# A hand-written instruction order, searched anew for a load in two parts

## The chip, the cores and the metric

One core of a Trainium2 chip runs the kernel. The metric is the device time of one execution in microseconds (us); lower is better. A profile of one execution tells when each instruction ran on each engine: PE (TensorE), DVE (VectorE), ACT (ScalarE), POOL (GpSimd) and SP (SyncE, which issues DMAs here).

## The reference

A layer norm of x (2048 tokens of 512, bf16) feeds two branches whose sum is added to x. Branch A is attention with 32 heads of 16 in four segments of 512 tokens: causal softmax inside the segment, plus a memory read of all earlier segments, mixed by a gate for each head. Branch B is a dense layer of width 1792 with silu.

```python
xn = layernorm(x)                                    # 2048 x 512
q, k, v = xn @ wq, xn @ wk, xn @ wv                  # 32 heads of 16
for s in range(4):                                   # segments of 512 tokens
    p = softmax(qs @ ks.T * 16 ** -0.5 + mask)       # causal within the segment
    a_mem = (phi(qs) @ M) / (phi(qs) @ z + 1e-6)     # phi(t) = t + 1 for t > 0, else exp(t)
    outs.append(g * a_mem + (1 - g) * (p @ vs))      # g = sigmoid(beta), one for each head
    M += phi(ks).T @ vs; z += phi(ks).sum(0)
return x + concat(outs) @ wo + silu(xn @ w1) @ w2
```

## The kernel before

The work is cut into small pieces, and one string, ORDER, lists all 1,349 of them in the order in which they are recorded. Each engine runs its own instructions in exactly that order; nothing is moved by a scheduler. A loop at the end of the function takes the words one by one and calls the function that PIECES names for them. So ORDER alone decides what stands ahead of what in each engine's queue, and how far a producer runs ahead of its reader.

The pieces that are spoken of below, with s for the segment:

- xc, xd, xs, xg, xq, xi, Nv: layer norm of one token tile (sums at L286, variance at L289, square root on ACT at L303 or on POOL at L297 and L300, reciprocal at L306, normalising at L315). X turns a tile on PE (L845), Xa and Xv copy it out (L851), XD turns it by DMA (L857).
- k, q, v, h: products with wk, wq, wv, w1; one word is a quarter of a 128x512 result in segments 0 and 1, half of one in segments 2 and 3. In segment 0 a word of k, q or h is two matmuls of 256 columns. kv, ka, qv, qa, vv, va copy a result from PSUM (v on DVE, a on ACT; L376, L399, L406). kp (L385, POOL) and kf split k into odd and even heads. ha is the tanh half of silu (ACT, L492), hv the rest (DVE, L497).
- fp, fa, fv and gp, ga, gv: phi of k and of q on POOL (L417, called pos), ACT (L423, called ex) and DVE (L433); t turns phi of k by DMA.
- S: scores of one batch (PE, L724), its exp on ACT (L730) and its causal masks on POOL (L744). The number is 18 s + 9 pair + batch. E and O: the weighted sums of v for the even and odd heads of four (PE, L791), copied by Ev, Ov, Ea, Oa (L821, L828), which also send the softmax sums to the tile zraw by small DMAs (L813); Om merges them (L835).
- s, sv, r, w, R, W: sums, their reciprocals (L545, L560) and gate weights (L566); z and d spread these over rows by DMA (L577); zv, dv multiply with them (L589, L599); m, n, nv are the memory's products (nv adds at L608).
- o, oc, od, oh: products with w2 and wo for one output tile (L336 or L338); st and sh store it (L621, L668). In o3.1.17 the numbers are segment, output tile, and the piece of the sum (14 to 17 are the attention's four quarters, below that the dense branch). xl loads x for the last sum. lw0 and lw1 load w2 and wo through ACT's queue.

Scores use a PSUM tile (psS) of one buffer; all other results share four banks (tag pb), so a product waits until the copy of the result that held its bank is done. A product stands in whole 128-column form (L336) or as four 32-column matmuls side by side (L338), by what tiled piece comes next in ORDER:

```python
psS = psatt.tile([P, 4, L], F32, name="psS")        # psatt: bufs=1
def bank(shape, dtype, name):
    return pp.tile(shape, dtype, name=name, tag="pb")   # pp: bufs=4
```

The loads at the start go through SP in this order: x, wv, wk, wq, x tiles 4 to 7, w1 in two halves of its columns, x tiles 8 to 15, beta.

Of the kernel before, what the change touches and what calls it, by code (L numbers as in the profile page):

```python
# [47 lines left out]
S31 o0.0.5 o0.2.14 h1.13.0 h1.13.1 o0.2.16 gv1.2 h1.13.2 o0.1.16 h1.13.3 ha1.13 fv1.1 o0.0.9 fp1.0
S30 oc0.1.9.1 od0.1.8.0 fp1.2 o0.1.5 o0.1.4 st0.0 h1.12.0 h1.12.1 h1.12.2 hv1.13 Nv13 XD13 h1.12.3 ha1.12 hv1.12 t1.1 o0.1.11 o0.3.17 o0.1.12
S33 fa1.2 oc0.1.9.0 kp2.0 o0.3.14 od0.3.3.1 od0.2.11.1 st0.2 oc0.3.0.0 o0.3.13 o0.3.10 E6 o0.1.6 o0.3.7  # L50
S32 o0.3.16 od0.1.8.3 oc0.3.2.0 mw0.2 o0.3.9 O6 o0.1.13 fv1.2 Ev6 oc0.3.0.1 o0.3.8 t1.2 Ov6 fa1.0 o0.1.15 fv1.0 od0.1.8.2
S35 o0.1.17 gp1.3 v2.0.0 o0.1.7 ga1.3 t1.0 o0.3.12 q2.2.0 q2.2.1 qv2.2
S34 od0.3.3.0 v2.0.1 vv2.0 o0.3.6 od0.3.3.2 ga2.1 Om6 o0.1.0 o0.3.1 E7 Ev7 o0.1.1
S41 o0.3.4 h1.5.0 O7 gv1.3 h1.5.1 h1.5.2 Ov7 od0.1.8.1 h1.5.3 gp2.1 o0.3.5 ha1.5 oc0.3.2.1
S37 o0.1.14 o0.3.15 hv1.5 m1.2 mv1.2 od0.3.3.3 o0.3.11 st0.3 k3.1.0 s1 gv2.1 sv1 r1.0 k3.1.1 gp2.3 r1.2 kv3.1 ga2.3
S36 o0.1.2 oc0.1.3.0 q3.3.0 q3.3.1 v2.3.0 qa3.3 v2.3.1 vv2.3 r1.3 gp2.2 xl0.1
S40 o1.2.13 r1.1 oc1.2.3.1 q3.1.0 m1.0 mv1.0 mw1.0 od1.2.1.1 oc0.1.3.1 o0.1.10 st0.1 w1 d1.0 d1.2 q3.1.1 qv3.1 o1.2.2 ga2.2
S43 oc1.2.11.1 z1.2 h1.6.0 h1.6.1 h2.8.0 Om7 h2.8.1 o1.2.4 ha2.8 hv2.8 h1.6.2 h1.6.3 od1.2.1.2 ha1.6
S38 E8 hv1.6 o1.2.9 o1.2.0 gv2.3 h2.11.0 h2.11.1 ha2.11 o1.2.10 o1.2.8
S42 gv2.2 v3.3.0 v3.3.1 Ev8 fp2.0 v3.0.0 v3.0.1 hv2.11 fa2.3 vv3.0 dv1.2 d1.1 k3.0.0 d1.3 fa2.0 k3.0.1 kv3.0 vv3.3 zv1.2  # L60
S39 q3.2.0 q3.2.1 qa3.2 fv2.0 z1.3 oc1.2.11.0 fp2.3 E9 q3.0.0 Ev9
S44 q3.0.1 k3.2.0 qv3.0 oc1.2.3.0 O8 fa2.1 fv2.3 Ov8 k3.2.1 kv3.2
S45 v3.2.0 v3.2.1 o1.0.9 gp3.2 fp2.1 mw1.2 fa2.2 dv1.3 xl1.0 zv1.3 h2.7.0 h2.7.1 vv3.2 o1.0.6 ha2.7 hv2.7 xl1.2
S48 o1.0.13 oc1.0.7.0 o1.0.4 h2.6.0 h2.6.1 Om5 n1.3 ha2.6 o1.2.12 kp2.3 o1.2.7 nv1.3 od1.2.1.0 oc1.0.10.0
# [878 lines left out]
```

## Time and profile before

| | before |
|---|---|
| median of 3 runs | 221.3 us (220.81 to 221.44) |
| profiled execution, its own time | 220.8 us |
| its span, first to last instruction | 219.1 us |
| granted TensorE clock | 1.0 |
| instructions in the profile | 9,343 |

The span is what the profile shows between the first and the last instruction; 1.7 us of the profiled execution's time lie outside it. Rows of an engine give the busy share of 40 equal slices in tenths. Times in rows of the timeline are us from the span's start, then the duration, then engine, line, operation and what it writes and reads. Matmuls overlap, so a row's duration holds the tail of the last one; the distance between starts tells the rate.

### The profile page before, as it was taken

What the parts mean: (1) busy time and instruction counts of PE and PEld (TensorE: products, weight loads), DVE (VectorE), ACT (ScalarE), POOL (GpSimd) and SP (SyncE); (2) the same over time, 40 slices, a digit from 0 to 9 for tenths busy, and PEclk for the clock granted to TensorE, in tenths of its full rate; (3) what the DMA queues carried; (4) which work ended last, traced back from release to release, by engine and by line L of the source; (5) the groups of instructions that cost most, each with busy time, mean ns of one, the idle gap of its engine ahead of it and who ended that gap; (6) DMA issues with size and microseconds to landing.
All of it is one profiled execution on the core that took longest, in us unless ns stands there. A gap on an engine that the chain in (4) does not pass through costs nothing.

```text
span 219.1 us, 9343 instructions
## 1 busy us (share of the span) xinstructions
PE 211.6 (97%) x4019; PEld 116.3 (53%) x4042; DVE 181.0 (83%) x370; ACT 184.2 (84%) x173; POOL 126.8 (58%) x203
## 2 busy tenths in 40 slices
PE   7999999999999999999999999999999999999994
...
DVE  7899999999897878757988979777899798669364
ACT  3899989999999999999999999999999988860000
POOL 6039986679687845695845486667768473410000
...
GB/s 197 357 372 128 79 129 344 42 79 46 4 4 75 25 86 71 83 62 29 51 74 61 43 121 28 47 79 7 4 99 75 75 76 45 97 60 76 97 52 97
DMA packets 33273, 19.60 MB, mean 89 GB/s; under 512 B 14672, under 2 KB 33232, under 8 KB 33232
## 3 DMA queue, kind: packets, MB, share of 16 engines
...
q14 instruction: 10, 0.08, 0.1%
...
## 4 chain that ended last, share of the span: by engine, by line
PE 82%; DVE 9%; POOL 4%; issue 2%; ACT 1%
PE ps L336 20%; PE psO L338 16%; PE ps L338 15%; PE psS L724 9%; PE psO L336 9%; PE psV L791 8%; PE psS L338 4%; DVE stats L286 2%; POOL Pb L744 2%; DVE Vz L406 1%; POOL k L385 1%; DVE hT L497 1%; DVE pk L433 1%; POOL lows L744 1%; PE ptr L845 1%
## 5 line engine op out<-in xcount | busy, mean ns | idle before, releaser
L730 ACT ACTIVATE Pb<-psS 128x2048 bf16<-128x2048 f32 x72 | 135.2, 1877 | 6.3 <-PE psS L724 4.1
L744 POOL TENSOR_SCALAR_AFFINE_SELECT Pb<-Pb 128x512 bf16<-128x512 bf16 (+2 forms) x88 | 61.6, 710 | 19.2 <-ACT Pb L730 16.5
L497 DVE SCALAR_TENSOR_TENSOR hT<-th,ps 128x512 bf16<-128x512 bf16 x56 | 38.0, 681 | 10.6 <-ACT th L492 10.2
L744 POOL TENSOR_SCALAR_AFFINE_SELECT lows<-Pb 64x512 bf16<-64x512 bf16 (+1 forms) x40 | 23.2, 581 | 37.5 <-ACT Pb L730 31.1
L338 PE MATMUL psO<-w_sb,hT 128*32 128x512 bf16 (+2 forms) x708 | 43.3, 321 | 0.0
L336 PE MATMUL ps<-xnT,w_sb 128*128 128x512 bf16 (+1 forms) x165 | 34.2, 329 | 0.4 <-DVE Vz L406 0.2
L492 ACT ACTIVATE th<-ps 128x512 bf16<-128x512 f32 x56 | 33.2, 594 | 1.7 <-PE ps L338 1.6
L338 PEld LDWEIGHTS <-hT 128*32 128x32 bf16 x876 | 21.6, 97 | 14.0 <-issue 2.6
L338 PE MATMUL ps<-xnT,w_sb 128*32 128x512 bf16 (+1 forms) x448 | 26.4, 348 | 0.0
L724 PE MATMUL psS<-qT,k 32*128 32x64 bf16 (+3 forms) x512 | 23.0, 233 | 0.5 <-ACT Pb L730 0.3
L336 PEld LDWEIGHTS <-w_sb 128*128 128x128 bf16 x168 | 15.8, 98 | 11.4 <-issue 1.0
L791 PE MATMUL psV<-Pb,Vz 128*32 128x448 bf16 (+7 forms) x512 | 21.6, 286 | 0.2 <-POOL Pb L744 0.2
L724 PEld LDWEIGHTS <-k 32*128 32x128 bf16 x512 | 9.4, 92 | 22.8 <-issue 22.2
L336 PE MATMUL psO<-w_sb,hT 128*128 128x512 bf16 (+2 forms) x82 | 20.9, 326 | 0.6 <-issue 0.5
L791 PEld LDWEIGHTS <-Vz 128*32 128x32 bf16 x768 | 16.2, 97 | 9.2 <-issue 0.8
L621 DVE SCALAR_TENSOR_TENSOR o_out<-psO,x_res 128x512 bf16<-128x512 f32 x14 | 9.6, 689 | 6.6 <-PE psO L338 4.9
L338 PEld LDWEIGHTS <-w_sb 128*32 128x32 bf16 x448 | 11.2, 96 | 7.3 <-issue 1.6
L724 PE MATMUL psS<-qT,kT 16*128 16x448 bf16 (+3 forms) x256 | 14.7, 269 | 0.0
L821 DVE CAST oraw<-psV 128x512 bf16<-128x512 f32 x15 | 10.2, 682 | 3.1 <-PE psV L791 3.0
L406 DVE CAST Vz<-ps 128x512 bf16<-128x512 f32 x15 | 10.2, 682 | 2.8 <-PE ps L338 1.6
L336 PEld LDWEIGHTS <-hT 128*128 128x128 bf16 x89 | 7.8, 98 | 8.7 <-issue 2.2
L336 PE MATMUL ps<-xnT,wq_sb 128*128 128x256 bf16 (+1 forms) x59 | 12.1, 322 | 0.2 <-issue 0.2
...
## 6 DMA issues: line engine op xcount, KB each, us to landing
...
```

Of the source, the lines that this page charges most:

```text
L286: nc.vector.bn_stats(out=stats[t][:], in_=xs(t, t + 1)[:, 0, :])
L336: return [nc.tensor.matmul(out, lhsT=lhsT, rhs=rhs, start=start, stop=stop, skip_group_check=True)]
L338: nc.tensor.matmul(out[c : c + 32], lhsT=lhsT[:, c : c + 32], rhs=rhs, start=start, stop=stop, tile_position=(0, c), skip_group_check=True,)
L406: copy(out=Vzs[s % 2][:, j, :, 0:3:2, :], in_=sts[s].pop(("v", j))[:, :].rearrange("p (h r d) -> p h r d", r=2, d=DH),)
L492: nc.scalar.activation(out=th[:], in_=sts[s]["h", ft][:, :], func=AF.Tanh, scale=0.5)
L497: nc.vector.scalar_tensor_tensor(out=st["hT"][:, ft, :], in0=st.pop(("th", ft))[:], scalar=1.0, in1=st.pop(("h", ft))[:, :], op0=ALU.add, ...
L621: out = nc.vector.scalar_tensor_tensor(out=o_out[:], in0=st.pop(("psO", j)), scalar=0.5, in1=st["x", j][:], op0=ALU.mult, op1=ALU.add)
L724: nc.tensor.matmul(psS[:, g, c : c + q2 - q1], lhsT=keys[rows], rhs=st["qT"][rows, dt, q1:q2], start=True, stop=True, tile_position=(32 * ...
L730: exp = nc.scalar.activation(out=blocks(Pb, b).rearrange("p y g c -> p g y c"), in_=psS[:, :, :].rearrange("p g (y c) -> p g y c", c=BLOCK ...
L744: over[id(Pb)].append(nc.gpsimd.affine_select(out=out, in_=in_, compare_op=ALU.is_ge, fill=0.0, base=base, pattern=[[0, out.shape[1]], [1, ...
L791: nc.tensor.matmul(psV[32 * g : 32 * g + 32, q0 : q0 + nq].rearrange("p (y c) -> p y c", y=weights.shape[2]), lhsT=Vzs[s % 2][:, kt, 4 * d ...
L821: copy(out=oraw[:], in_=sts[s].pop(("psV", 0))[:, :])
```

## The change

Only ORDER changes: the same pieces in another order. A search over orders was run again with the loads as the kernel has them, w1 in two parts. Four copies change their engine: kv0.1 becomes ka0.1, qa3.2 and qa3.3 become qv3.2 and qv3.3, and Ev14 becomes Ea14 (a is ACT, v is DVE). The S words stand in the same order, and what stands between them differs in nearly every line. The diff, cut to the lines that matter:

```diff
--- before
+++ after
 ORDER = """
-kind odd omask ones0 ones1 zeros xc0 xd0 xc1 xq0 xi0 Nv0 busy44 xd1 xq1 xc2 xi1 X0.1 Nv1 xd2 Xa0.1 busy6 v0.0.0 v0.0.1 xq2 X1.1 Xa1.1 xs3 xi2 Nv2 v0.0.2 xq3 v0.0.3 xi3 v0.1.0 v0.1.1 Nv3 X2.1 va0.0 k0.0.0 k0.0.1 tb Xv2.1 X3.1 v0.1.2 v0.1.3 Xv3.1 vv0.1 k0.1.0 k0.0.2 k0.0.3 ka0.0 fp0.0 kf0.0 q0.0.0 q0.0.1 q0.0.2 q0.0.3 xs4 k0.1.1 qa0.0 k0.1.2 k0.1.3 kv0.1 fa0.0 xs7
-S0 k0.3.0 fa0.1 k0.2.0 k0.2.1 k0.2.2 k0.2.3 kv0.2 k0.3.1 k0.3.2 q0.1.0 xs5 xs6 xg4.4 fv0.0 k0.3.3 kv0.3
-S2 q0.1.1 v0.2.0 kp0.1 q0.1.2 q0.1.3 qv0.1 v0.2.1 v0.2.2 v0.2.3 vv0.2 fa0.2 Nv6 Nv4 XD6 XD4 h0.0.0 h0.0.1
-S1 Nv5 XD5 h0.0.2 h0.0.3 ha0.0 hv0.0 h0.1.0 h0.1.1 fp0.2 h0.1.2 h0.1.3 q0.2.0
-S3 q0.2.1 q0.2.2 q0.3.0 q0.3.1 q0.3.2 q0.2.3 Nv7 qv0.2 ha0.1 h0.2.0 h0.2.1 kp0.2 q0.3.3
-S4 qv0.3 hv0.1 XD7 fv0.2 fa0.3 h0.2.2 v0.3.0 v0.3.1 v0.3.2 t0.0 t0.2 xs10 h0.3.0 h0.3.1 h0.3.2 h0.4.0 fp0.3 h0.3.3 ha0.3 v0.3.3
-S7 vv0.3 fp0.1 hv0.3 h0.4.1 h0.4.2 h0.4.3 kp0.3 h0.2.3 v1.2.0 ha0.4 v1.2.1 xs13 tanh E0 Ev0
-S5 v1.2.2 v1.2.3 h0.5.0 hv0.4 h0.5.1 h0.5.2 ha0.2 h0.5.3 vv1.2 fv0.3 O0 Ov0
-S11 lw0 hv0.2 xs11 q1.1.0 q1.1.1 q1.1.2 v1.1.0 v1.1.1 v1.1.2 v1.1.3 q1.1.3 q1.2.0 lw1
-S6 vv1.1 q1.2.1 q1.2.2 q1.2.3 v1.3.0 v1.3.1 v1.3.2 qv1.1 ga1.1 xs8 qv1.2 v1.0.0 v1.0.1 xs9 xg8.4 v1.0.2 v1.0.3 vv1.0 v1.3.3 ha0.5 hv0.5 t0.3
...
-S13 q1.3.1 q1.3.2 Nv9 q1.3.3 qv1.3 k1.2.3 Nv11 XD11 h0.9.0 h0.9.1 Om1 h0.9.2 h0.9.3 h0.10.0 ha0.9 hv0.9 kv1.2 kp1.2
...
-S15 k1.1.2 h1.0.0 h1.0.1 h1.0.2 k1.1.3 h1.0.3 ha1.0 xs14 E2 kv1.1 XD10 Ev2
-S17 O2 Ov2 h1.10.0 h1.10.1 h1.10.2 kp1.1 xl0.2 m0.2 mv0.2 h1.10.3 m0.0 ha1.10 mv0.0 hv1.0 fp1.3
...
-S14 ha0.12 xs12 k2.1.0 hv0.11 Om0 gp1.0 h1.3.1 k2.1.1 kv2.1 hv0.12 q2.1.0 q2.1.1
-S16 xg12.4 k2.2.0 k2.2.1 h1.3.2 h0.13.0 qv2.1 kv2.2 h1.3.3 Om2 E3 ha1.3
...
-S24 hv0.13 o0.2.7 oc0.2.10.1 od0.2.11.2 fv1.3 h1.8.0 h1.8.1 Nv15 XD15 h1.8.2 h1.8.3 h1.11.0 h1.11.1 h1.11.2 ha1.8
...
-S23 h1.4.0 oc0.0.7.1 o0.2.9 o0.0.6 h1.4.1 o0.0.1 Nv12 Ov4 h1.4.2 h1.4.3 ha1.4 od0.0.0.1 o0.0.4 bmask gv1.0 od0.0.0.2
-S25 h1.9.0 h1.9.1 kp2.1 Om3 zv0.3 h1.9.2 XD12 h1.9.3 ha1.9 oc0.2.10.0 hv1.4 o0.2.12 XD14 E5 zv0.1 o0.2.15
...
-S51 n1.0 o1.2.15 h2.4.0 h2.4.1 ha2.4 od1.2.1.3 nv1.0 o1.0.14 od1.0.1.0 fv2.2 t2.3 t2.2 o1.2.14 o1.2.16 st1.2
-S50 k3.3.0 k3.3.1 ga2.0 hv2.4 kp3.0 kv3.3 ga3.2 O10 Ov10 od1.0.1.3 o1.0.15 st1.0 h2.2.0 h2.2.1 ha2.2 o1.1.9 hv2.2
-S52 h2.9.0 kp3.1 m2.0 h2.9.1 ha2.9 o1.1.13 mv2.0 o1.1.1 od1.1.6.0 gv3.2 gp2.0 E11 hv2.9
-S56 o1.3.8 oc1.3.4.1 od1.3.9.2 Om9 o1.3.7 o1.1.16 Ev11 o1.1.14 od1.1.6.1 O11 Ov11 o1.1.3 kp3.2 Om10 o1.3.2 ga3.0
...
-S64 o2.2.10 xl2.0 hv3.8 od2.0.6.3 s3 o2.0.17 o2.2.3 sv3 r3.1 dv2.1 h3.9.0 h3.9.1 ha3.9 od2.0.6.1 dv2.2 r3.0 od2.2.13.0
...
-S71 hv3.13 o2.1.12 o2.3.4 h3.3.0 o2.3.9 h3.3.1 h3.10.0 h3.10.1 ha3.3 oc2.3.5.0 ha3.10 o3.2.5 o3.2.11 hv3.3 oh1.0 oc2.1.0.1 o3.2.8 o3.2.7 hv3.10 h3.6.0 oh5.1 h3.6.1 ha3.6 xl3.0 od2.3.10.2 O15 R0.3 d3.1 oc2.1.0.0 o2.1.13 oh13.0 R0.0 Oa15 o3.2.1 R0.2 oh7.0 dv3.0 oc2.1.3.1 o3.2.0 o3.0.5 hv3.6 o2.3.6 oh2.1 o3.1.2 o3.1.7 dv3.1 oc3.0.0.0 o3.0.11 R0.1 W0 oh13.1 od2.3.10.0 o3.0.9 o2.1.1 oc2.1.3.0 o3.2.13 o3.2.10 dv3.3 od3.0.3.3 o3.1.13 o2.3.3 Om15 o3.1.8 o3.1.1 o2.3.14 od3.0.3.0 o2.3.16 o2.3.17 xl2.3 R1.3 o3.1.6 o3.1.9 z3.2 o3.0.13 R1.1 od3.1.0.0 od2.1.9.1 R1.0 R1.2 W1 oh6.0 o2.3.8 Om14 zv3.2 o3.0.8 oc3.0.0.1 oc3.1.10.1 o2.3.7 o2.1.11 oc3.0.12.0 o3.0.7 z3.0 dv3.2 oh0.1 z3.1 od2.1.9.0 o2.3.12 z3.3 o3.2.2 o2.1.8 o2.1.4 st2.1 o3.2.4 o2.3.1 od2.3.10.3 o3.2.12 o3.1.4 oc3.1.10.0 od3.0.3.1 n3.0 oc3.1.11.1 od2.3.10.1 od3.1.0.1 o2.3.13 zv3.0 oh10.0 nv3.0 xl3.1 o3.0.4 oc2.3.2.0 o3.2.3 o2.3.0 o3.0.14 o3.2.6 oc2.3.5.1 st2.3 n3.2 oh3.0 xl3.2 oh2.0 zv3.3 oh11.0 od3.1.0.2 oh10.1 nv3.2 o3.0.1 oc3.1.11.0 o3.1.12 zv3.1 oh9.1 o3.1.14 oh14.1 oc3.0.12.1 o3.2.9 oh8.1 n3.1 nv3.1 o3.2.14 o3.1.3 n3.3 oh14.0 o3.0.16 od3.0.3.2 oh4.1 oh0.0 o3.1.15 o3.2.16 oh5.0 o3.1.16 nv3.3 o3.0.2 o3.0.17 o3.0.6 o3.0.10 o3.0.15 st3.0 o3.2.17 o3.2.15 oh6.1 st3.2 od3.1.0.3 oh8.0 oh16.1 o3.1.17 o3.1.5 oh12.0 oh17.1 oh9.0 st3.1 oh7.1 oh15.0 oh17.0 oh4.0 oh16.0 sh0 oh12.1 oh3.1 oh15.1 oh11.1 oh1.1 sh1
+kind odd omask ones0 ones1 zeros xc0 xd0 xc1 xq0 xi0 Nv0 busy44 xd1 xq1 xc2 xi1 X0.1 Nv1 xd2 Xa0.1 busy6 X1.1 xq2 v0.0.0 v0.0.1 v0.0.2 Xa1.1 v0.1.0 v0.1.1 xs3 xq3 xi2 Nv2 v0.0.3 X2.1 xi3 Nv3 v0.1.2 X3.1 v0.1.3 Xv2.1 k0.0.0 tb k0.0.1 Xv3.1 k0.0.2 vv0.1 va0.0 k0.0.3 ka0.0 kf0.0 q0.0.0 xs4 xs7 q0.0.1 q0.0.2 q0.0.3 k0.1.0 qa0.0 bmask k0.1.1 k0.1.2 fa0.0 fp0.0 fv0.0 t0.0
+S0 k0.2.0 k0.2.1 xs6 xs5 xg4.4 k0.1.3 ka0.1 fp0.1 v0.2.0 v0.2.1 v0.2.2 q0.1.0 q0.1.1 q0.1.2 kp0.1
+S2 v0.2.3 fa0.1 k0.2.2 k0.2.3 k0.3.0 k0.3.1 kv0.2 k0.3.2 k0.3.3 q0.1.3 vv0.2 qv0.1 kv0.3 kp0.3 Nv6
+S1 h0.0.0 h0.0.1 h0.0.2 h0.0.3 XD6 h0.3.0 ha0.0 v0.3.0 v0.3.1 Nv5 XD5 v0.3.2 h0.1.0
+S3 Nv4 h0.1.1 h0.1.2 hv0.0 v0.3.3 vv0.3 h0.3.1 h0.3.2 XD4 h0.3.3 h0.2.0 ha0.3 h0.1.3 xs10 hv0.3
+S4 fv0.1 h0.2.1 h0.2.2 q0.3.0 q0.3.1 q0.3.2 q0.3.3 Nv7 q0.2.0 fp0.3 q0.2.1 q0.2.2 q0.2.3 ha0.1 XD7 t0.1 fa0.2 qv0.3
+S7 hv0.1 h0.4.0 qv0.2 h0.4.1 h0.4.2 h0.2.3 ha0.2 h0.4.3 kp0.2 xs9 fp0.2 E0 Ev0 v1.2.0
+S5 tanh v1.2.1 v1.2.2 hv0.2 xs11 v1.2.3 v1.1.0 v1.1.1 vv1.2 h0.5.0 v1.1.2 v1.1.3 vv1.1 ha0.4 hv0.4 xs8 xg8.4 h0.5.1
+S11 h0.5.2 h0.5.3 ha0.5 O0 q1.1.0 Ov0 q1.1.1 q1.1.2 q1.1.3
+S6 k1.2.0 k1.2.1 qv1.1 k1.2.2 ga1.1 hv0.5 lw0 fv0.2 v1.3.0 v1.3.1 q1.2.0 v1.3.2 v1.3.3 vv1.3 k1.2.3 kv1.2 Nv8 XD8 q1.0.0
...
+S13 k1.1.1 O1 Ov1 h0.9.0 h0.9.1 h0.9.2 h0.9.3 h0.10.0 ha0.9 xs15
...
+S15 h1.0.0 h1.0.1 xs13 kv1.1 h1.0.2 hv0.10 qv1.3 h1.10.0 h1.10.1 xl0.2 E2 Ev2 h1.0.3 ha1.0 hv1.0 h1.10.2 xs12
+S17 h1.10.3 k1.3.0 ha1.10 k1.3.1 k1.3.2 xg12.4 k1.3.3 kv1.3 O2 h0.12.0
...
+S14 lw1 h0.11.1 k2.2.0 k2.2.1 kv2.1 kv2.2 q2.1.0 q2.1.1 hv0.12
+S16 h1.3.0 h1.3.1 h1.3.2 kp1.2 qv2.1 h0.11.2 Om1 h0.11.3 m0.0 mv0.0 h1.3.3 ha1.3 ha0.11 Nv15 E3 Ev3
...
+S24 q2.3.0 q2.3.1 mw0.0 Ov3 Nv13 hv0.13 h1.8.0 h1.8.1 h1.8.2 h1.8.3 vv2.1 kp1.3 ha1.8 o0.2.7
...
+S23 xl0.0 h1.4.0 h1.4.1 o0.0.1 gp1.0 h1.4.2 od0.2.11.3 o0.2.17 od0.0.0.3 o0.0.4 h1.4.3 Om2 zv0.2 ga1.2 ha1.4 oc0.0.2.1 o0.2.12
+S25 o0.0.5 o0.2.16 hv1.4 h1.9.0 h1.9.1 h1.9.2 o0.0.11 oc0.0.7.0 o0.0.3 h1.9.3 ha1.9 gv1.0 E5 od0.2.11.0
...
+S51 o1.0.15 n1.0 xl1.1 t2.1 h2.4.0 h2.4.1 kp3.0 nv1.0 fa2.2 o1.2.16 o1.2.14 oc1.2.11.1 o1.2.7 st1.2 ha2.4 O10 xl1.3
+S50 k3.3.0 k3.3.1 Ov10 od1.0.1.2 h2.2.0 h2.2.1 hv2.4 xl1.0 ha2.2 o1.0.14 kv3.3 fv2.2
+S52 t2.2 o1.3.8 ga3.3 h2.9.0 od1.3.9.1 o1.3.0 kp3.2 od1.3.9.0 hv2.2 o1.3.13 o1.1.9 oc1.1.10.1 od1.3.9.2 od1.1.6.1 fv2.0 t2.0 h2.9.1 ha2.9 hv2.9
+S56 oc1.1.10.0 o1.1.5 gp2.0 o1.1.13 o1.3.1 o1.3.10 o1.1.11 ga2.0 oc1.0.10.0 st1.0 o1.1.1 E11 Ev11 o1.3.6 kp3.3 Om10
...
+S64 o2.0.3 hv3.8 o2.0.10 o2.0.14 n2.3 nv2.3 o2.0.12 od2.0.6.3 h3.9.0 h3.9.1 ha3.9 s3 oc2.0.5.0
...
+S71 o2.3.7 E15 Ev15 oc2.1.3.1 h3.10.0 h3.10.1 ha3.10 oc2.1.0.1 xl2.3 od2.3.10.0 hv3.10 o2.3.14 h3.6.0 Om14 h3.6.1 oh4.1 o2.3.0 ha3.6 oh7.0 oh0.1 o3.2.2 oh1.1 O15 o3.2.9 hv3.6 o3.2.5 oh2.1 Oa15 o2.3.9 o3.1.2 o3.1.5 o3.1.3 o3.1.9 xl2.1 dv3.2 o2.3.4 o3.0.5 o2.3.1 oc3.0.0.0 R0.2 od3.0.3.2 o2.1.15 od3.1.0.2 R0.3 R0.1 o3.1.12 oc3.1.10.0 R0.0 W0 z3.2 oc3.0.12.0 o2.3.6 o2.3.12 dv3.3 o3.0.7 dv3.1 o3.2.1 od3.1.0.1 oh9.1 R1.1 od3.0.3.0 z3.0 o2.1.14 oc2.3.2.0 oc3.0.0.1 R1.0 o2.3.17 o3.1.7 oc2.3.5.1 od2.3.10.3 oc3.1.10.1 o3.0.10 R1.2 o3.0.11 st2.3 oh0.0 o2.1.2 R1.3 oh7.1 o3.1.4 oh1.0 od2.1.9.2 o3.1.1 o2.1.10 o2.1.6 W1 oh12.1 n3.2 oh2.0 o3.0.6 oh8.0 zv3.2 o3.0.2 oh10.0 o3.2.11 od3.0.3.1 z3.3 z3.1 od3.0.3.3 od3.1.0.3 dv3.0 nv3.2 oh16.0 od2.1.9.3 zv3.0 o3.2.3 od3.1.0.0 o3.1.8 o3.1.16 o3.1.6 st2.1 xl3.2 o3.2.0 o3.1.13 oh10.1 n3.0 nv3.0 n3.3 xl3.3 oh4.0 o3.0.4 o3.0.1 o3.0.8 oh13.0 oh6.0 Om15 o3.2.10 o3.2.14 n3.1 o3.1.14 o3.0.16 o3.2.16 oh11.1 zv3.3 oh3.0 oh11.0 oh12.0 nv3.3 o3.1.17 o3.2.7 oh14.1 o3.0.9 oh9.0 oc3.1.11.1 oc3.0.12.1 zv3.1 nv3.1 o3.0.14 o3.1.15 o3.2.15 o3.0.17 oh17.0 o3.0.15 o3.0.13 st3.0 oc3.1.11.0 st3.1 oh14.0 oh15.0 o3.2.13 o3.2.4 oh5.0 o3.2.8 oh13.1 o3.2.12 o3.2.6 o3.2.17 sh0 st3.2 oh5.1 oh3.1 oh17.1 oh6.1 oh15.1 oh8.1 oh16.1 sh1
 """
```

More of the change, by code (lines that the diff above doesn't have):

```diff
@@ L48 @@
[L48 to L64, printed above, removed]
```

81 lines of the change are left out of this document (49 added, 32 removed).

## The prediction

> **What bounds the kernel now.** I read the profile's page first, then the costliest groups, the waits of PE, and the order of time in the stage where PE's row has its low digits.
>
> ```profile
> span 219.1 us, 9343 instructions
> PE 211.6 (97%) x4019; PEld 116.3 (53%) x4042; DVE 181.0 (83%) x370; ACT 184.2 (84%) x173; POOL 126.8 (58%) x203
> PE   7999999999999999999999999999999999999994
> DVE  7899999999897878757988979777899798669364
> ACT  3899989999999999999999999999999988860000
> POOL 6039986679687845695845486667768473410000
> ```
>
> PE is busy to the end; ACT is full until slice 34, DVE most of all in slices 3 to 12, POOL in slices 4 and 5. The ACT groups say what paces the list: 72 exps of 1.88 us, and beside each about one shorter piece.
>
> ```profile
> L730 ACT ACTIVATE Pb<-psS 128x2048 bf16<-128x2048 f32 x72 | 135.2, 1877 | 6.3 <-PE psS L724 4.1
> L492 ACT ACTIVATE th<-ps 128x512 bf16<-128x512 f32 x56 | 33.2, 594 | 1.7 <-PE ps L338 1.6
> L423 ACT ACTIVATE ex<-kT 128x512 bf16<-128x512 bf16 x12 | 7.4, 622 | 0.0
> ```
>
> The scores tile psS has one buffer, so a scores pass S on PE waits for the exp of the S before it. The timeline of S2, S1 and S3 shows that cycle:
>
> ```profile
> 14.47 0.40 PE L724 MATMUL psS<-qT,k 32*128 32x64 bf16 x8
> 14.92 1.88 ACT L730 ACTIVATE Pb<-psS 128x2048 bf16<-128x2048 f32 x1
> 16.33 0.60 PE L336 MATMUL ps<-xnT,w_sb 128*128 128x256 bf16 x4
> 16.86 0.21 PE L724 MATMUL psS<-qT,k 32*128 32x64 bf16 x4
> 17.20 1.48 PE L336 MATMUL ps<-xnT,w_sb 128*128 128x256 bf16 x12
> 19.25 0.40 PE L724 MATMUL psS<-qT,k 32*128 32x192 bf16 x8 [0.35 <-ACT Pb L730]
> ```
>
> S2 starts at 14.47, its exp at 14.92 (0.45 later), lasts 1.88, and S1 starts 0.06 after its end: no two S can start closer than 2.39 us. PE fills that time with pieces of the list. Twelve 256-column matmuls start at 17.20 and the two after them end at 18.74, so 0.11 each and 0.22 for a piece of segment 0 (two of them). S itself takes 0.34 (16.86 to 17.20), and about 0.10 goes before it (four matmuls from 16.33 end at 16.77; S1 starts at 16.86). Nine pieces make 9 x 0.217 + 0.43 = 2.38 us, just the cycle. Between S1 and S3 the list has seven: 1.95 us, 0.44 short, and PE waits (0.35 in the row, which leaves out the matmuls' tail).
>
> The other waits that PE has:
>
> ```profile
> PE psS L724 <- ACT Pb L730: 0.3, 1, 0.3
> PE psV L791 <- POOL Pb L744: 0.2, 1, 0.2
> PE ps L336 <- DVE Vz L406: 0.2, 1, 0.2
> ```
>
> There is little left to win: PE's work is the same in both lists, so only waits, and the time before PE is fed, can change. No load of w1 stands among PE's waits.
>
> **The change part by part.** The same 1,349 pieces stand in both lists, but for four copies that change engines: kv0.1 goes to ACT, two q copies of segment 3 go from ACT to DVE, and the even copy of E14 goes to ACT. ACT has two copies fewer and two more. Both lists hold 72 S, 37 changes from whole tiles to S and 35 from column tiles to S, so tile changes cost the same. The terms, against the profiled 220.8 us (span 219.1 and 1.7 around it; 0.5 below the median of 221.3):
>
> *Start.* The first S waits for a chain through four tiles of x:
>
> ```profile
> 6.31 0.41 DVE L315 TENSOR_SCALAR xn_t<-x_lo,mv_all,rstd_all 128x512 bf16<-128x512 bf16 x1
> 6.91 0.39 PE L845 MATMUL ptr<-ident,xn_t 128*128 128x128 bf16 x4
> 7.86 0.31 ACT L303 ACTIVATE rstd_all<-mv_all,eps 128x1 f32<-128x1 f32 x1
> 8.20 0.16 DVE L306 RECIPROCAL rstd_all<-rstd_all 128x1 f32<-128x1 f32 x1
> 12.07 0.21 PE L724 MATMUL psS<-qT,k 32*128 32x64 bf16 x4 [0.16 <-ACT qT L399]
> ```
>
> Tile 1 is normalised by 6.72, but X1.1 stands behind two v pieces and runs at 6.91. The new list has X1.1 ahead of them: it can start at 6.78, 0.13 sooner, and the copies on ACT, xq3 (7.86), xi3 (8.20), Nv3, X3.1 and the k and q copies follow. S0: 11.94 instead of 12.07, **-0.13** (0 if DVE holds xi3, which is free only at about 8.03, so -0.17 at most). The table load (tb) now stands ahead of va0.0 on ACT; both end before ka0.0 is due. k0.1.3 moves behind S0: one piece more after it, **+0.22**.
>
> *Short intervals.* Counted as above from the two lists, before: S1-S3 0.44, S7-S5, S5-S11 and S15-S17 0.10 each, S17-S21 0.08, S24-S18 0.06, S64-S68 0.05, others under 0.03 each 0.18: 1.11 us. After: S2-S1 and S3-S4 0.22 each (eight pieces), S7-S5, S11-S6, S13-S12, S17-S21 0.10 each, others 0.13: 0.97 us. **-0.14**. Where two short ACT pieces stand between exps, the exp starts late by what exceeds the 0.5 us gap; in the new list the next interval is long enough each time (S16-S19-S24, S23-S25-S29, S52-S56-S61), by 0.04 to 0.1 us.
>
> *E0.* It waits for S4's mask on POOL:
>
> ```profile
> 14.53 0.41 POOL L744 TENSOR_SCALAR_AFFINE_SELECT lows<-Pb 64x256 bf16<-64x256 bf16 x1 [2.67 <-ACT Pb L730]
> 16.10 0.57 POOL L297 TENSOR_SCALAR rstd_all<-mv_all 128x4 f32<-128x4 f32 x1 [0.45 <-DVE mv_all L289]
> 21.88 0.61 POOL L417 TENSOR_SCALAR pos<-kT 128x512 bf16<-128x512 bf16 x1
> 23.32 1.02 POOL L385 TENSOR_SCALAR k<-kT,pm_odd 128x512 bf16<-128x512 bf16 x1
> 24.32 0.47 POOL L385 TENSOR_SCALAR k<-kT,pm_even 128x256 bf16<-128x256 bf16 x1
> 25.59 1.09 POOL L744 TENSOR_SCALAR_AFFINE_SELECT Pb<-Pb 128x1024 bf16<-128x1024 bf16 x1
> 25.92 0.61 PE L791 MATMUL psV<-Pb,Vz 128*32 128x512 bf16 x12
> 26.73 0.29 PE L791 MATMUL psV<-Pb,Vz 128*32 128x256 bf16 x4 [0.20 <-POOL Pb L744]
> 49.06 0.54 PE psV L791 x16
> ```
>
> Sixteen matmuls of an E take 0.54 (last row, of the chain), so the last four were due at 26.33 and came at 26.73: 0.40 lost. POOL worked from S0's mask (14.53) to S4's (26.68) for 12.15 us with 0.45 idle. In the new list one pos (0.61) of that queue goes behind S4's mask, and on DVE the four statistics stand ahead of two k copies, so the 0.45 that POOL waited for them mostly goes: POOL could be through at 14.40 (S0's exp, 11.94 + 2.33, and 0.13) + 12.15 - 0.61 - 0.4 = 25.5. S4's exp ends at 23.83 (S4 at 21.5, four cycles after 11.94, + 2.33), and its two masks then need 0.13 + 1.89 (24.79 to 26.68): 25.85. E0 starts 1.42 after S7 (24.1) and reads it 0.41 later, 25.93. **-0.4** to 0; I take **-0.3**.
>
> *v1.1.0.* It takes the bank that the first odd copy frees:
>
> ```profile
> 29.69 0.82 PE L336 MATMUL ps<-xnT,wq_sb 128*128 128x512 bf16 x2
> 29.84 0.68 DVE L828 CAST odd<-psV 128x512 bf16<-128x512 f32 x1
> 30.57 1.02 PE L336 MATMUL ps<-wv_sb,xnT 128*128 128x512 bf16 x4
> ```
>
> Three q pieces from 29.69 end at 30.34 (one record is missing); v1.1.0 starts 0.05 after the copy's end: 0.22 lost. The new list has v1.1.0 ahead of O0: **-0.2**.
>
> *New waits.* Every piece changes neighbours, so some bank or mask will be late elsewhere: k3.3.0 now stands 0.99 us of PE work behind o1.2.7, and the bank that it needs comes free after a store of 0.69 and some 0.25 of drain and signals. Bounds: nothing, and 1.2 us, twice what the two waits above lost. I take **+0.3**, near the smaller rows.
>
> *Loads and tail.* lw0 moves by one S and lw1 to S14; both weights are first read long after, and the issue runs beside an ACT piece. After S71 the new list has 23.3 us of PE work, the old 25.2, so the chain that ends in the last products has less cover:
>
> ```profile
> 197.43 0.54 DVE L560 RECIPROCAL ri<-zraw 96x64 f32<-96x64 bf16 x1
> 198.01 0.35 DVE L566 TENSOR_SCALAR rz<-ri,gate 96x256 bf16<-96x256 f32 x1
> 198.82 0.66 SPq L577 DMA_DIRECT2D spr<-rz  x1
> 202.14 0.42 DVE L589 TENSOR_TENSOR oT<-spr,oraw 128x512 bf16<-128x512 bf16 x1
> ```
>
> In the new list W1 stands behind st2.3, which waits for o2.3.17, 10.5 us after S71 in PE work. From there: store 0.7, two reciprocals 1.1, W1 0.35, the spread z3.3 some 3.3 (198.82 to 202.14 for one with both its issues), zv3.3 0.42, nv3.3 0.7: 17.1. The first product that reads it stands at 18.2. Nothing, with 1.1 us in hand.
>
> Sum: -0.13 + 0.22 - 0.14 - 0.3 - 0.2 + 0.3 = -0.25, about -0.3 us: 220.5 for a profiled run, 221.0 for the median. 0.3% (0.66 us, the spread of the runs shown) is about what a measurement can tell from no change.
>
> **The rivals.** *Faster by more:* the list's new waits don't come and S0 gains fully. -0.17 + 0.22 - 0.14 - 0.4 - 0.22 = -0.7, 220.6; with short intervals that vanish because the 2.39 is met elsewhere, up to 1 us more: 219.6. For it: the old waits named are local and their causes are moved. Against: both lists are about equally tight; several pieces stand within 0.2 us of their bank.
>
> *Slower: POOL becomes the bound at S11.* kp0.2, which S11 reads, now stands behind S7's mask. S7's exp stands behind a th and an ex (23.83 + 0.59 + 0.62) and ends at 26.9, the mask takes 0.13 + 0.66, kp0.2 then 1.47 by its rows (23.32 to 24.79), to 29.2; S11 is due at 29.4 (26.9 + 0.06 + 2.39). It decides when POOL runs over 0.2 us late here; each further 0.1 is lost, by E0 first and by S11 again. At 0.7 late in both, +0.5 and +0.5 over the sum: 222.0. For it: the odd half of kp took 1.02 here. Against: S4's exp, not POOL's queue, ends last before E0. [...]
>
> *It doesn't do what it says:* the order is meant for w1 in two parts, and no wait on w1 shows; then it is only another order, with the forecast's time.
>
> **How the numbers follow.** Forecast (waits moved, little net) 0.48; faster rival beyond 0.3% 0.32; POOL rival or another late producer of its size 0.20. Most of the doubt is in the new waits. Range: from 219.6 (faster rival's end) to 222.5 (the slower one with 0.5 more for the upper bound of new waits).
>
> **What would show it.** After: S0 at about 11.94; E0's matmuls without a POOL gap; S1 and S4 waiting 0.2 us each for an exp and S3 not; no wait at the first v piece after O0. Wrong, if PE shows a new wait over 0.3 us, above all at S11 or in a stage after 40 us, or if S0 does not move. PE's busy work must be the same.

## The result

| | before | after |
|---|---|---|
| median | 221.25 us (220.79 to 221.44, 6 runs) | 222.06 us (221.93 to 222.78, 6 runs) |
| ratio after : before | | 1.0046, 95% interval 1.0028 to 1.0063 |
| profiled execution, its own time | 220.8 us | 221.93 us |
| its span | 219.1 us | 220.2 us |
| granted TensorE clock | 1.0 | 1.0 |

The searched list is slower by 0.8 us, and the interval of the ratio lies wholly above 1; 221.0 was forecast. On the page after, PE's busy share is 97% as before:

```profile
span 220.2 us, 9304 instructions
...
PE 212.7 (97%) x3999; PEld 116.8 (53%) x4024; DVE 180.9 (82%) x370; ACT 184.7 (84%) x173; POOL 127.9 (58%) x203
...
POOL 6049875767769743998575465797756562420000
```

POOL's row has moved: 9 9 8 in slices 17 to 19 (some 88 to 104 us), where the old list has 6 9 5. PE's timeline of the start and of the first intervals after:

```profile
11.95 0.21 PE L724 MATMUL psS<-qT,k 32*128 32x64 bf16 x4 [0.16 <-ACT qT L399]
...
14.35 0.40 PE L724 MATMUL psS<-qT,k 32*128 32x64 bf16 x8
...
16.73 0.21 PE L724 MATMUL psS<-qT,k 32*128 32x64 bf16 x4
...
19.14 0.40 PE L724 MATMUL psS<-qT,k 32*128 32x192 bf16 x8
...
25.58 0.73 PE L791 MATMUL psV<-Pb,Vz 128*32 128x512 bf16 x16
26.12 0.40 PE L338 MATMUL ps<-wv_sb,xnT 128*32 128x512 bf16 x4
...
29.06 0.40 PE L724 MATMUL psS<-qT,k 32*128 32x64 bf16 x8
```

S0 stands at 11.95 and S2, S1, S3 follow at the cycle. E0's sixteen matmuls (25.58) end when the next piece starts, 0.54 later: the gap of 0.40 is gone. S11 stands at 29.06, 0.30 us earlier than in the old list, and S8 at 34.04 instead of 34.78. But by its S8 the new list has run two pieces (0.217 us each) fewer than the old one, so of these 0.74 us only 0.3 are a lead.

Then it loses. PE's waits after, and the place of the largest one (first PE, then POOL, then ACT):

```profile
PE psV L791 <- POOL Pb L744: 0.4, 1, 0.4
```

```profile
100.68 0.72 PE L791 MATMUL psV<-Pb,Vz 128*32 128x512 bf16 x16
101.43 0.40 PE L338 MATMUL ps<-xnT,w_sb 128*32 128x512 bf16 x4
...
102.09 0.61 PE L338 MATMUL psO<-w_sb,hT 128*32 128x512 bf16 x8
103.12 0.62 PE L791 MATMUL psV<-Pb,Vz 128*32 128x448 bf16 x16 [0.41 <-POOL Pb L744]
```

```profile
99.26 0.62 POOL L417 TENSOR_SCALAR pos<-qT 128x512 bf16<-128x512 bf16 x1
99.83 1.23 POOL L744 TENSOR_SCALAR_AFFINE_SELECT Pb<-Pb 128x256 bf16<-128x256 bf16 x2
101.13 0.69 POOL L385 TENSOR_SCALAR k<-kT,pm_odd 128x512 bf16<-128x512 bf16 x1
101.80 0.48 POOL L385 TENSOR_SCALAR k<-kT,pm_even 128x256 bf16<-128x256 bf16 x1
102.23 0.83 POOL L744 TENSOR_SCALAR_AFFINE_SELECT Pb<-Pb 128x512 bf16<-128x512 bf16 x1
```

```profile
99.61 1.88 ACT L730 ACTIVATE Pb<-psS 128x2048 bf16<-128x2048 f32 x1 [0.56 <-PE psS L724]
```

S34's exp ends at 101.49. Its mask could run then, but kp2.3 (101.13 and 101.80) stands ahead of it on POOL, and POOL's rows have followed each other within 0.1 us since 94.86. The mask ends at 103.06 and O7's first matmul that reads it is at 103.12: the eight matmuls before it are through at 102.53, so 0.59 us are lost (0.41 in the row, which leaves out the matmuls' tail). In the old list POOL stands idle for 0.65 us ahead of the same mask, the mask takes 0.66 instead of 0.83, and O7 follows on it (POOL, then PE of before):

```profile
100.30 0.66 POOL L744 TENSOR_SCALAR_AFFINE_SELECT Pb<-Pb 128x512 bf16<-128x512 bf16 x1 [0.65 <-ACT Pb L730]
```

```profile
101.06 0.61 PE L791 MATMUL psV<-Pb,Vz 128*32 128x448 bf16 x16
```

So 0.17 of the 0.59 are the mask's own slower run, the rest is the queue. E7, just before in the new list, shows a smaller wait: sixteen matmuls of 0.54 from 100.68, and the next piece at 101.43 instead of 101.22.

The tail, DVE and then SP (stores) after, then DVE and SP of before:

```profile
216.19 0.42 DVE L668 SCALAR_TENSOR_TENSOR o_half<-psS,x_res 128x256 bf16<-128x256 f32 x1 [0.55 <-PE psS L338]
216.53 0.68 DVE L621 SCALAR_TENSOR_TENSOR o_out<-psS,x_res 128x512 bf16<-128x512 f32 x1
217.12 0.41 DVE L668 SCALAR_TENSOR_TENSOR o_half<-psS,x_res 128x256 bf16<-128x256 f32 x1
```

```profile
216.64 0.33 SPq L672 DMA_DIRECT2D out_dram<-o_half  x1
217.24 0.33 SPq L626 DMA_DIRECT2D out_dram<-o_out  x1
217.66 0.38 SPq L672 DMA_DIRECT2D out_dram<-o_half  x1
```

```profile
215.59 0.97 DVE L668 SCALAR_TENSOR_TENSOR o_half<-psS,x_res 128x256 bf16<-128x256 f32 x2 [0.18 <-PE psS L338]
```

```profile
214.19 1.58 SPq L626 DMA_DIRECT2D out_dram<-o_out  x3
216.05 0.88 SPq L672 DMA_DIRECT2D out_dram<-o_half  x2
```

PE ends at 216.90 after and at 216.09 before. After, DVE still has the full-width sum of o3.2 (0.68) ahead of the last half, and its store ahead of the last store: SP's last issue ends 1.14 us behind PE's end, before 0.84; the span ends 3.32 us behind it, before 2.99.

Counting every interval's matmuls at the prediction's rates, the span's 1.1 us is made of: start -0.12; one more piece after S0 +0.22; waits between S0 and S71, 2.54 us instead of 1.83, +0.71; tail +0.3. The 0.71 is a gain of 0.4 up to S8 and a loss of 1.1 behind it. The start is one execution's: in the five other runs that keep the old list up to S0, S0 stands at 12.16 to 12.47, in the six that keep the new one at 11.94 to 12.06.

### The profile page after: what moved, and what is told of

The parts are those of the page before. It is cut to its first block, busy times and chain, and to the rows that moved or that the text cites. A ratio compares the mean times of both kernels' runs of the same rounds, so it can differ in the third digit from the quotient of the medians.

```text
span 220.2 us, 9304 instructions
## 1 busy us (share of the span) xinstructions
PE 212.7 (97%) x3999; PEld 116.8 (53%) x4024; DVE 180.9 (82%) x370; ACT 184.7 (84%) x173; POOL 127.9 (58%) x203
## 4 chain that ended last, share of the span: by engine, by line
PE 73%; DVE 10%; ACT 7%; POOL 6%; issue 2%; DVEq 0%; POOLq 0%
PE ps L336 17%; PE ps L338 14%; PE psO L338 14%; PE psO L336 9%; PE psS L724 9%; PE psV L791 6%; ACT Pb L730 5%; PE psS L338 3%; POOL Pb L744 3%; DVE stats L286 2%; POOL k L385 2%; DVE hT L497 2%; DVE xn_t L315 1%; ACT th L492 1%; POOL lows L744 1%
## 5 line engine op out<-in xcount | busy, mean ns | idle before, releaser
L338 PE MATMUL psO<-w_sb,hT 128*32 128x512 bf16 (+2 forms) x628 | 39.5, 333 | 0.0
L336 PE MATMUL ps<-xnT,w_sb 128*128 128x512 bf16 (+1 forms) x142 | 32.0, 337 | 0.3 <-DVE qT L399 0.2
L338 PE MATMUL ps<-xnT,w_sb 128*32 128x512 bf16 (+1 forms) x528 | 29.2, 336 | 0.1
L336 PE MATMUL psO<-w_sb,hT 128*128 128x512 bf16 (+2 forms) x106 | 24.2, 308 | 0.6 <-issue 0.3
L336 PEld LDWEIGHTS <-w_sb 128*128 128x128 bf16 x148 | 13.2, 98 | 11.7 <-issue 2.4
L338 PEld LDWEIGHTS <-w_sb 128*32 128x32 bf16 x528 | 13.5, 96 | 8.1 <-issue 2.2
L336 PEld LDWEIGHTS <-hT 128*128 128x128 bf16 x109 | 10.0, 98 | 10.3 <-issue 1.4
L621 DVE SCALAR_TENSOR_TENSOR o_out<-psO,x_res 128x512 bf16<-128x512 f32 x14 | 9.5, 687 | 5.9 <-PE psO L338 4.6
L336 PE MATMUL ps<-xnT,wk_sb 128*128 128x256 bf16 (+1 forms) x59 | 12.9, 322 | 0.2
L828 DVE CAST odd<-psV 128x512 bf16<-128x512 f32 x15 | 10.3, 684 | 3.3 <-PE psV L791 3.3
L336 PE MATMUL ps<-wv_sb,xnT 128*128 128x512 bf16 x41 | 12.1, 379 | 0.3 <-issue 0.2
```

Source lines behind the costliest of these rows:

```text
L336: return [nc.tensor.matmul(out, lhsT=lhsT, rhs=rhs, start=start, stop=stop, skip_group_check=True)]
L338: nc.tensor.matmul(out[c : c + 32], lhsT=lhsT[:, c : c + 32], rhs=rhs, start=start, stop=stop, tile_position=(0, c), skip_group_check=True,)
L621: out = nc.vector.scalar_tensor_tensor(out=o_out[:], in0=st.pop(("psO", j)), scalar=0.5, in1=st["x", j][:], op0=ALU.mult, op1=ALU.add)
L828: copy(out=odd[:], in_=sts[s].pop(("psV", 1))[:, :])
```

## The experiments

Three theories were set against each other. W: PE's work is fixed, so the time is the start, PE's single waits, and what follows its last product; the loss is O7's wait, some bank waits, and the tail. C: the exps pace the list, so a wait that is taken away moves to the next scores pass. E: the early part loses, and pays later. The old list ran beside each group at 221.12, 221.05 and 220.94 us; the changed list ran only once, beside 221.25.

**One POOL word back** (late_kp23).

```diff
-S35 od0.3.3.0 q2.2.0 q2.2.1 o0.1.0 kp2.3 qv2.2 ...
-S34 ... E7 h1.5.0 Ev7 fa1.0 gp1.3
+S35 od0.3.3.0 q2.2.0 q2.2.1 o0.1.0 qv2.2 ...
+S34 ... E7 h1.5.0 Ev7 fa1.0 gp1.3 kp2.3
```

> The changed list with one word moved: kp2.3 (POOL, two instructions of 1.17 us together) goes from ahead of S34's mask to behind gp1.3, so that S34's mask can run when its exp ends. Theory W (the time is the start, plus PE's work, plus PE's waits, plus what follows PE's last product; the loss is a sum of single waits): the 0.59 us that PE lost ahead of O7 goes, the mask ends near 102.4 in the old profile's time, and the kernel takes 221.5 us, 0.6 below the changed list's 222.06. Rival C (the exps on ACT pace the list there, so that a wait taken away only moves to the next scores pass): under 0.2 us gained, and the excess appears ahead of S37 or S36. Rival P (the late part is slow by contention of DVE and POOL as a whole, not at one place): 222.0, and another POOL or DVE wait of like size shows after 100 us.

221.52 us (221.44 to 221.98), 0.54 less than the changed list's median. Against the old list beside each it is 0.40 above instead of 0.81, and the ratios' intervals (1.0017 to 1.0035, 1.0028 to 1.0063) overlap, so the trace has to carry the cause. The mask now waits for its exp alone, and O7 follows without a gap (POOL, then PE):

```profile
101.61 0.66 POOL L744 TENSOR_SCALAR_AFFINE_SELECT Pb<-Pb 128x512 bf16<-128x512 bf16 x1 [0.51 <-ACT Pb L730]
```

```profile
102.15 0.61 PE L338 MATMUL psO<-w_sb,hT 128*32 128x512 bf16 x8
102.59 0.61 PE L791 MATMUL psV<-Pb,Vz 128*32 128x448 bf16 x16
```

W foretold this place. C falls: S37, the next scores pass behind O7, stands 0.54 earlier than in the changed list. P of the expectation falls too: no other wait of that size follows. But 0.17 us come back ahead of s1, which starts at 107.98, right behind two sums of DVE (L621, 106.65 to 107.92). Ahead of them a merge on DVE took 0.87 instead of 0.45, while a mask on POOL beside it and beside an L433 sum took 1.14 instead of 0.64; that these caused it wasn't tried. In this profiled execution the start is 0.10 later as well, and 0.13 go between S58 and S57, where the list is unchanged (tail_sh0, with the same words there, loses 0.16). So PE ends only 0.24 us earlier than in the changed list's trace: differences of 0.1 to 0.2 us between two traces need not come from the edit.

**The tail** (tail_sh0).

```diff
-... oh15.0 o3.2.13 o3.2.4 oh5.0 o3.2.8 oh13.1 o3.2.12 o3.2.6 o3.2.17 sh0 st3.2 oh5.1 ...
+... oh15.0 oh5.0 sh0 o3.2.13 o3.2.4 o3.2.8 o3.2.12 o3.2.6 o3.2.17 st3.2 oh13.1 oh5.1 ...
```

> The changed list with its last 25 words rearranged: oh5.0 ends the first half of the last tile earlier, sh0 stands right behind it and ahead of o3.2.17's store, and oh13.1 goes behind st3.2. PE's work is the same. Theory W: sh0 runs some 0.5 us earlier, st3.2 follows right after o3.2.17, sh1 starts within 0.1 us of PE's end instead of 0.2 behind it, and its store is issued alone: 0.3 us less, 221.75. Rival D (the last store's own way through the queue sets the end, whatever stands ahead of it): under 0.1 us, 222.0.

221.76 us (221.52 to 222.72), 0.30 less at the median; as a time that isn't clear of the spread (its ratio to the old list lies in 1.0018 to 1.0052, the changed list's in 1.0028 to 1.0063), and the trace decides. DVE's rows show sh0 0.55 us earlier and the last half right behind PE's end (216.99):

```profile
215.64 0.42 DVE L668 SCALAR_TENSOR_TENSOR o_half<-psS,x_res 128x256 bf16<-128x256 f32 x1
216.17 0.69 DVE L621 SCALAR_TENSOR_TENSOR o_out<-psS,x_res 128x512 bf16<-128x512 f32 x1
217.04 0.42 DVE L668 SCALAR_TENSOR_TENSOR o_half<-psS,x_res 128x256 bf16<-128x256 f32 x1 [0.18 <-PE psS L338]
```

From PE's end to the span's end it is 3.00 us, as in the old list (2.99), where the changed list has 3.32.

**Two splices** (early_after: the changed list up to S24, the old one from there; late_after: the reverse).

```diff
 (early_after)
 S14 lw1 h0.11.1 k2.2.0 ... q2.1.1 hv0.12 fa1.3
 ...
 S24 Ov3 hv0.13 vv2.1 gp1.0 kp2.2 Om2 o0.2.7 oc0.2.10.1 ...
```

> A splice: the changed list up to S24, the old list from S24 on (the words that one half had and the other lacked are put at the seam; fa1.3 into S14's line). Theory W: start -0.12, one more piece +0.22, waits up to S24 1.16 instead of 1.42 us; S24 comes 0.15 us earlier than in the old list, the rest is as in the old list: 221.1 us, 0.15 below the old list's 221.25 (0.0 to 0.3 below). Rival E (the early part is where the changed list loses, since POOL and DVE are behind there and pay later): 221.9 or more.

> The other splice: the old list up to S24, the changed list from S24 on, with its tail. Theory W: it has the old list's early waits (1.42 us to S24) and the changed list's late ones (1.38 against the old list's 0.41), and the changed tail (+0.3): 221.25 + 0.97 + 0.31 = 222.5 us (222.2 to 222.7), slower than both lists. Rival E (the early part loses): 221.4.

early_after: 221.48 us, 0.36 above the old list where 0.15 below was expected. Yet PE does what W says: S24 comes at 61.68 (old list 61.86) and PE ends at 215.91, 0.18 ahead of the old list's 216.09. The loss is on SP, behind PE's end; the tail's order is the old list's word for word, but its issues are not:

```profile
208.99 2.10 SPq L614 DMA_DIRECT2D x_res<-in_A_x_dram  x1
214.02 2.29 SPq L626 DMA_DIRECT2D out_dram<-o_out  x3
216.40 0.89 SPq L672 DMA_DIRECT2D out_dram<-o_half  x2
```

Three stores from 214.02 take 2.29 instead of 1.58, so both last stores go out late (from 216.40 instead of 216.05). The DMA view of 214.2 to 214.8 us of the same kernel shows what is new there:

```profile
q8 instruction: 1, 0.02, 10.8%
q14 instruction: 1, 0.01, 5.2%
```

The first row is a load of instructions of 16 KB. The old list's page has `q8 instruction: 31, 0.51, 1.0%`: with 4,042 weight loads and 4,019 matmuls on PE, one load for some 260 of them. That these loads are PE's is taken from this count, and from the runs below in which more instructions on PE move them. In early_after they fall at 209.2 and 214.4 (loads are timed to 0.2 us), beside the load of x above, which takes 2.10 instead of 0.43, and the store of o3.2, which takes 1.21 instead of 0.34. In the old list they fall at 207.1 and 212.0, between SP's issues. The load on q14 is in the old list too, at 214.6, among the same stores. This made a new theory, F: an issue on SP that meets PE's instruction load is held up, and at the end of the kernel that is paid in full.

late_after: 224.12 us against 222.5 expected, by a fault of the seam. DVE had a queue of bmask, gate and two normalisations ahead of hv0.13, and PE stood until that was through (the trace is of an execution of 226.25 us, the longest of the five; the expectation below names hv1.8):

```profile
67.18 2.55 PE L336 MATMUL ps<-xnT,w_sb 128*128 128x512 bf16 x6 [2.29 <-DVE hT L497]
```

A second version with those words elsewhere (late_after2) still lost there, some 2 us between 65 and 74 us, and one of its last stores met an instruction load at 217.8:

> The second splice (the old list up to S24, the changed one from there) with a mended seam: bmask and gate are made earlier, Nv13 and Nv15 stand behind hv1.8 and hv1.11, so that DVE's queue no longer holds up hv1.8, which cost 2.36 us of PE at the seam before. Theory W: the old list's early waits, the changed list's late ones (0.97 us more than the old list's) and its tail (0.31): 222.4 us (222.0 to 222.7), above both lists. Rival E (the changed list loses in its early part): 221.3.

It took 224.82 us, and as times both are inconclusive. Its trace does bear on E: behind the old list's early part the changed late part loses just what it lost in the changed list, 1.23 us of waits from S28 to S71 (changed list 1.22, old list 0.36), with the same wait at O7:

```profile
105.65 0.62 PE L791 MATMUL psV<-Pb,Vz 128*32 128x448 bf16 x16 [0.41 <-POOL Pb L744]
```

**Instruction loads** (early_forms, old_forms, old_forms_half). The form of 20 words is changed, in early_after (early_forms) and in the old list (old_forms): four 32-column matmuls for one of 128 columns, three more matmuls and three more weight loads a word, 120 instructions in all. An estimate from the two traces: at one load for some 260 instructions, and 5.2 and 4.9 us between the last two loads, 120 instructions bring a load 2.4 and 2.3 us forward, from 214.4 to 212.0 in early_after and from 212.0 to 209.7 in the old list, where the next one then stands at 214.6. The work's time is the same (PE's end moves by 0.03 and 0.1 us); the instruction loads move. The half dose has the second range alone.

```diff
-        narrow[0] = now == "cols"
+        narrow[0] = now == "cols" or 518 <= i < 532 or 546 <= i < 566
```

> The first splice (the changed list up to S24, the old one from there) with 20 words of two intervals (o0.0.14 to o0.0.16, oc0.1.9.1 to o0.1.12) as four 32-column matmuls instead of one whole matmul each: same columns, same streaming time, 120 more instructions on PE. [...] Theory F (an issue on SP that meets PE's instruction load is held up, and at the end this is paid in full): 120 instructions bring the loads 2.4 us forward, to 206.8 and 212.0; the last store's issue goes back to 0.34, and the time falls by 0.4 to 0.5 us to 221.0. Rival G (the forms themselves cost, or the slow issue has another cause): 221.5 or more.

> [...] Theory F: the instruction loads move from 207.1 and 212.0 to about 209.7 and 214.6, where the last three stores are issued; one of these takes 0.7 us longer and the kernel 0.3 to 0.5 us: 221.5. Rival G (forms cost or not by themselves): 221.1 if they are free, and no slow issue in the tail.

The two cross: early_forms took 220.68 us (221.48 without the edit), old_forms 222.02 (221.05 without). SP's stores of early_forms, and of old_forms with the DMA view of its 214.6 to 215.2 us:

```profile
214.05 1.58 SPq L626 DMA_DIRECT2D out_dram<-o_out  x3
```

```profile
214.31 2.33 SPq L626 DMA_DIRECT2D out_dram<-o_out  x3
```

```profile
q8 instruction: 1, 0.02, 13.8%
```

The load stands at 212.0 in the first, at 214.8 in the second. F holds, and G falls: one and the same edit gains in one list and costs in the other. The size was set too low: 0.80 and 0.97 us at the median. The profiled executions differ by 0.50 and 0.68 us, and show 0.71 and 0.75 in these stores.

For the half dose the last loads were expected at 205.4 and 210.7:

> The old list with 11 of the 20 words (oc0.1.9.1 to o0.1.12) in 32-column form: 66 instructions more on PE. Theory F: the last instruction loads stand at about 205.4 and 210.7 us, none meets the last stores, and the time is the old list's, 221.1. Rival G (the forms cost by themselves, as their number): half of what the 20 words cost, 221.5.

It took 222.25 us. The loads are at 205.2 and 210.4, but a further one follows at 216.0, some 0.3 us ahead of PE's end (216.39), and it meets the last two stores (SP; 0.88 in the old list):

```profile
216.35 1.55 SPq L672 DMA_DIRECT2D out_dram<-o_half  x2
```

The expectation missed the third load; the row is what F says, on another store, and it explains 0.67 of the 0.98 us by which the profiled execution is longer than the old list's. The other 0.3 are there at S0 already (12.39 instead of 12.07), and what the rest of the median's 1.3 is stays open. As a time, 222.25 fits neither F's 221.1 nor G's 221.5. In the old and in the changed list the last load (212.0 and 212.7) meets none of the last stores, so F has no part in the result.

**All waits of the changed list treated** (after_mended): the first two edits, and four words moved within their lines.

```diff
-S10 ... vv1.0 Om0 k1.1.0 ha0.7 hv0.7
+S10 ... vv1.0 k1.1.0 ha0.7 hv0.7 Om0
-S22 ... r0.2 w0 ha1.1 hv1.1 z0.2 ...
+S22 ... r0.2 ha1.1 hv1.1 w0 z0.2 ...
-S32 O6 gv1.2 Ev6 ga1.3 o0.3.5 o0.1.4 ...
+S32 gv1.2 Ev6 ga1.3 o0.3.5 O6 o0.1.4 ...
-S35 ... o0.1.6 gv2.3 o0.1.14 v2.0.0
-S34 v2.0.1 o0.1.12 vv2.0 o0.3.6 ...
+S35 ... o0.1.6 o0.1.14 v2.0.0
+S34 v2.0.1 o0.1.12 vv2.0 gv2.3 o0.3.6 ...
```

> The changed list with all its single waits treated: kp2.3 behind gp1.3 and the new tail as in the two runs before, and Om0 behind hv0.7 (0.24 ahead of h0.10.0), w0 behind hv1.1 (0.13 ahead of E4), O6 behind o0.3.5 (0.16), gv2.3 behind vv2.0 (0.20 ahead of h1.5.0). Theory W: 222.06 - 0.55 - 0.3 - 0.6 = 220.6 us, below both lists. Rival C (the small bank waits only move to the next neighbour): 221.2, what the first two edits give.

220.87 us (220.69 to 221.75), 1.19 below the changed list and 0.18 below the old one (ratio 0.9998, 0.9988 to 1.0009: no difference from the old list, and clear of the changed list's 1.0028 to 1.0063). By the medians the first two edits make 0.84 of it by their own runs and the four words some 0.35; the trace gives the words 0.51 up to S41, of the 0.6 expected. Three of the four do what they should (0.07 is left ahead of S12). The move of w0 gains nothing: E4 now starts without a wait at 70.50, but its last four matmuls come at 71.12, behind POOL's mask (69.89 to 71.06), and that interval loses 0.20 us where it lost 0.16. Behind O7, 0.2 come back ahead of s1, as in late_kp23. In these two places the rival holds, that a wait only moves on.

**The reverse, in the old list** (old_kp23): kp2.3 from S48's line to the place behind gp1.3, ahead of S34's mask.

```diff
-S35 o0.1.17 gp1.3 v2.0.0 ...
+S35 o0.1.17 gp1.3 kp2.3 v2.0.0 ...
```

> The old list with kp2.3 moved from S48's line to right behind gp1.3, ahead of S34's mask: the reverse of the first edit. In the old list POOL has 0.65 us idle ahead of that mask, the mask ends at 100.96 and O7 starts at 101.06 without a wait. kp2.3 takes 1.17 on POOL, so the mask comes 0.52 later. Theory W: O7's last matmuls wait 0.5 us and the kernel takes 221.6 us, 0.5 more than the old list. Rival C (the exps pace the list there): 221.2.

222.17 us, 1.23 above the old list, twice what was expected. PE, POOL and DVE:

```profile
102.18 0.62 PE L791 MATMUL psV<-Pb,Vz 128*32 128x448 bf16 x16 [0.86 <-POOL Pb L744]
```

```profile
99.83 0.79 POOL L385 TENSOR_SCALAR k<-kT,pm_odd 128x512 bf16<-128x512 bf16 x1
100.60 0.47 POOL L385 TENSOR_SCALAR k<-kT,pm_even 128x256 bf16<-128x256 bf16 x1
101.03 1.10 POOL L744 TENSOR_SCALAR_AFFINE_SELECT Pb<-Pb 128x512 bf16<-128x512 bf16 x1
```

```profile
100.89 0.72 DVE L433 SCALAR_TENSOR_TENSOR phiQT<-ex,pos 128x512 bf16<-128x512 bf16 x1
```

The mask comes late as foretold, and on top takes 1.10 instead of 0.66; its later place lies beside DVE's phi sum (100.89 to 101.61). O7 loses 1.03 us: some 0.6 by the queue and 0.44 by the slow mask. PE's end is 1.07 us later than in the old list's trace.

**The best list** (best_splice): early_forms with Om0 behind hv0.7.

> The first splice with the 20 words in 32-column form (220.68 us, its last instruction load clear of the stores), and one word more: Om0 behind hv0.7, so that DVE frees h0.10.0's bank in time (0.24 us of PE at 43.6). Theory W: 0.2 us less, 220.45, faster than the old list by 0.6 us. Rival C (the wait moves to S12 or S15): 220.65.

220.54 us (220.46 to 222.16), ratio to the old list 0.9982 (0.9966 to 0.9999): below both lists, the old one by 0.40 us where W said 0.6, less than 0.3% and at the edge of the interval. In the trace the wait ahead of h0.10.0 falls by 0.18 us and doesn't come back.

## Why the prediction was wrong

- *Start*: right. S0 at 11.95, 11.94 foretold; the extra piece cost its 0.22.
- *Short intervals*: right. S3's 0.43 is gone; S1 and S4 wait 0.20 us each.
- *E0*: right in kind. S4's mask ends at 25.79 (25.85 foretold) and E0 waits for nothing. But S5 is still 0.13 us late behind S7's exp, which two short ACT pieces hold back to 24.74; 0.16 was gained there, not 0.3.
- *v1.1.0*: right; its wait is gone.
- *New waits*, +0.3 with bounds 0 and 1.2: this is the step that failed, a term set at a quarter of what it measured. The trace after has 1.50 us of them (0.24 ahead of h0.10.0, 0.15 at E4, 0.09, 0.16 behind O6, 0.21 behind E7, 0.59 at O7, 0.06), and some 0.35 us of the like in the old list's late part goes: some 1.2 net, the upper bound itself. Of the 1.36 us between the forecast's -0.25 and the span's +1.11, this term has 0.9, the tail 0.33 and E0 0.14. The prediction's own sign of being wrong, a new wait over 0.3 us after 40 us, is O7's. The bounds came from the waits that the old list shows, which say nothing of the new list's places. The order gave the largest place away: kp2.3 moved forward over twelve scores passes, to ahead of S34's mask, into a queue that was full (1.23, 0.62 and 1.17 us stand between 99.26 and 102.23), and old_kp23 shows that this one move costs 1.0 us of PE even in the old list.
- *Loads and tail*, "nothing": wrong by 0.3. The chain of the last normaliser was indeed covered; what was not looked at were the last copies on DVE and SP: o3.2's full-width sum, 216.53 to 217.21, and its store stand ahead of the last half, though PE ends at 216.90.
- *Rival "POOL becomes the bound"*: the mechanism was the right one, a kp ahead of a mask, but at S11 it didn't strike (S11 at 29.06, no wait); it struck at S34's mask, 73 us later, with one loss of 0.59 instead of two of 0.5. That its 222.0 is close to the measured 222.06 is luck, as the rest came from smaller waits and the tail. POOL's pieces do run longer beside some of DVE's L433 sums: the mask in old_kp23 1.10 us against 0.66, and the 128x256 half of kp 0.90 to 0.97 in the four rows of both lists that lie beside one, against 0.47 to 0.65 in the 26 others. Why was not shown.
- *Rival "faster by more"*: by the same count it had 0.3 of its 0.7 us at S8, and the waits up to E7 had spent them before O7.
